# Attention in a fused kernel: normalising two steps later, the first round of products with values in two parts, weight conversions in other steps

## The chip, the cores and the metric

The kernel runs on one core of a Trainium2 chip. The metric is device time in microseconds (us) of one execution. Engines: TensorE (PE; PEld is its weight load), VectorE (DVE), ScalarE (ACT), GpSimd (POOL) and SyncE (SP), which issues DMA transfers. Each engine works through its own queue in order.

## What is computed

Threshold attention over 4 batches of 8 heads with 576 positions and a head width of 64, then two feed-forward layers over the 2304 tokens. Only the attention stands nearer here:

```python
scores = scale * np.matmul(q, k.transpose(0, 1, 3, 2))
thresh = np.max(scores, axis=-1, keepdims=True) - tau
scores = np.where(scores >= thresh, scores, -1000000000.0)
scores = scores - np.max(scores, axis=-1, keepdims=True)
attn = np.exp(scores)
attn = attn / (np.sum(attn, axis=-1, keepdims=True) + 1e-09)
return np.matmul(attn, v).astype(np.float32)
```

The feed-forward layers are `(1 / (1 + exp(-(x @ w_gate))) * (x @ w_val)) @ w_out` and a second one with a piecewise quadratic gate.

## The kernel before

Attention goes over 16 pairs of heads (`NP`). Each pair has five steps (`U` = 5): in steps 1 to 4 (`u` = 0 to 3) 128 queries of both heads, in step 5 (`u` = 4) the last 64 of both, through block-diagonal `corners`. The loop `for t in range(N + 9)` (L418) runs over all 80 steps and is a software pipeline: the code of one `t` issues parts of different steps.

- `scores(p, u)` (L243): TensorE writes the scores of step t into two PSUM tiles `wa` and `wb` (tile name w).
- `maxima` (L256): VectorE scales them into SBUF (tile s) and reduces them to the row maximum mx (L261); GpSimd adds tau to it (L264). The two PSUM tiles are free for the next scores once L261 has read them.
- `exponents` (L269): ScalarE, L273, tile ex.
- `masks` of step t - 1 (L276): VectorE compares, multiplies and sums (L281, tile p); GpSimd copies the last 64 columns into a tile lt (L288).
- `turns` of step t - 2 (L290): TensorE transposes p and lt (L298, L300, L317) into the PSUM tiles `wt` and `left`; `copies` (L322): ScalarE moves them into SBUF (tiles r and rl).
- `attend` (L343): the products with values, in two rounds. Round 0 takes the first 256 queries, round 1 the other 320; each is a sum over five chunks of 128 keys (the fifth is rl), in one PSUM tile `av`, which `drain` moves to `xall` on ScalarE (L359) after the last chunk. The table `rounds` (L412) says at which step after a pair's start which chunks of which round are issued; step 5 there is the first step of the next pair.
- The row sums are inverted (`denom`), transposed (L436), written to DRAM (`sum_rows`, L370) and read back on all partitions (`spread`, L376, tile rb) at the end of the tenth step after a pair's start. `normalise` (L378) multiplies `xall` by rb on GpSimd (L380), in two halves, in the twelfth and the thirteenth.

Beside that the loop converts the first feed-forward weights to single precision. `background` (L382) is a list of 43 pieces, one a call: an `extract` on ScalarE (L145) or one operation of VectorE on 128x512 elements (L155 to L169), and two loads ahead. L456 takes one piece in each of the second, third and fourth step of a pair up to step 62, and later yields a "gap" at the same places, in which the feed-forward part's first splits run on VectorE (L192, L506). L468 takes some extra ones.

No scheduler moves anything: each queue holds the work in the order in which the code issues it. At step 81 the loop yields to the feed-forward part, which issues its first weight loads (tile words, L129); TensorE's first products of that part follow (L514).

Of the kernel before, what the change touches and what calls it, by code (L numbers as in the profile page):

```python
# [29 lines left out]
def kernel(  # L30
# [21 lines left out]
    NP, _, S = q.shape  # L52
# [147 lines left out]
    def attention():  # L200
# [14 lines left out]
        U = nf + 1  # L215
# [27 lines left out]
        def scores(p, u):  # L243
            t = qk[p]
            for s in range(2):
                c = slice(s * HS, s * HS + HS)
                if u == nf:
                    nc.tensor.matmul(wa[:, s, :HS], corners[p % 2], t[:, 1, c], start=True, stop=True)
                    continue
                for e, w in enumerate((wa, wb)):  # L250
                    es = slice(e * D, e * D + D)
                    nc.tensor.matmul(  # L252
                        w[:, s, :HS], t[es, 0, u * P : u * P + P], t[es, 1, c], start=True, stop=True
                    )

        def maxima(p, u):  # L256

            t = sp.tile([P, 2, 2, HS], F32, tag="s", name="s")
            mx = mxs[(p * U + u) % 2]
            for e, w in enumerate((wa, wb)[: 1 if u == nf else 2]):  # L260
                nc.vector.tensor_scalar(  # L261
                    t[:, e], w[:, :, :HS], nscale, None, op0=ALU.mult, op1=ALU.min, accum_out=mx[:, 0, e : e + 1]
                )
                nc.gpsimd.tensor_scalar(  # L264
                    mx[:, 1, e : e + 1], mx[:, 0, e : e + 1], tau_b, None, op0=ALU.add
                )
            st[p, u] = t, mx

        def exponents(p, u):  # L269
            t, mx = st[p, u]  # L270
            ex = pe_.tile([P, 2, 2, HS], F32, tag="ex", name="ex")
            for e in range(1 if u == nf else 2):
                nc.scalar.activation(ex[:, e], t[:, e], AF.Exp, scale=-1.0, bias=mx[:, 0, e : e + 1])  # L273
            st[p, u] = t, mx, ex
# [15 lines left out]
        def turns(p, u):  # L290


            pr = pt.pop((p, u))
            if u == 2:
                for e in range(2):
                    for c in range(nf):
                        cs = slice(c * P, c * P + P)
                        nc.tensor.transpose(wt[:, e, cs], pr[:, e, cs], ident)  # L298
                for i in range(3):
                    nc.tensor.transpose(left[:, (i + 1) * P : (i + 2) * P], last(p, i), ident)  # L300
                return

            es = range(1 if u == nf else 2)
            todo = [(i * R, pr[:, e, c * P : c * P + P]) for i, (e, c) in enumerate(itertools.product(es, range(nf)))]
            if u == nf:
                todo.append((len(todo) * R, last(p, u)))
            for i, (o, x) in enumerate(todo):
                for h in range(2):
                    turn_half(wt[:, h, o : o + R], x, h)
                if u == 3 and i == 6:  # L310
                    turn_half(left[:, :R], last(p, 3, False), 0)
                if u == nf and i == 3:
                    turn_half(left[:, R:P], last(p, 3), 1)
# [8 lines left out]
        def copies(p, u):  # L322
            r, o = min(u // 2, 1), u % 2 * P if u < nf else 2 * P
            x = rt[r].rearrange("p e c n -> p (e c) n")
            if u == 2:
                nc.scalar.activation(x[:, :, o : o + P], wt.rearrange("p e (c n) -> p (e c) n", n=P), AF.Copy)
                nc.scalar.activation(rl[0], left[:, P : 3 * P], AF.Copy)
                nc.scalar.activation(rl[1][:, :P], left[:, 3 * P :], AF.Copy)
            elif u < nf:
                nc.scalar.activation(  # L330
                    x[:, :, o : o + P].rearrange("p m (h q) -> p h m q", h=2),
                    wt.rearrange("p h (m q) -> p h m q", q=R), AF.Copy,
                )
            else:
                nc.scalar.activation(
                    rt[r][:, :, :, o : o + R], wt[:, :, : nf * R].rearrange("p e (c q) -> p e c q", q=R), AF.Copy
                )
                nc.scalar.activation(rl[1][:, P : 2 * P], left[:, :P], AF.Copy)
                for e in range(2):
                    es = slice(e * R, e * R + R)  # L340
                    nc.scalar.activation(rl[1][es, o : o + R], wt[es, e, nf * R : (nf + 1) * R], AF.Copy)

        def attend(p, r, cs):  # L343


            n = NR[r]
            for c in cs:
                for e in range(2):
                    nc.tensor.matmul(  # L349
                        av[e * D : e * D + D, :n], vs[p % 3][:, e, c], rt[r][:, e, c] if c < nf else rl[r],  # L350
                        start=c == 0, stop=c == nf,
                    )

        def x_of(p):
            b, hp = divmod(p, NHP)
            return xall[:, hp, b * S : (b + 1) * S]
# [4 lines left out]
        def denom(p):  # L361
            rs = sums[p % 2]
            nc.vector.reciprocal(rs, rs)

        def sum_rows(p):

            n = 2 * nf + 1
            nc.scalar.activation(rows[p % 2][:n], left[:n, :P], AF.Copy)
            drs[p] = dram.tile([n, P], F32, tag="dr", name="dr")
            nc.sync.dma_start(out=drs[p], in_=rows[p % 2][:n])  # L370
# [7 lines left out]
        def normalise(p, s):  # L378
            x, c = x_of(p), slice(s * HS, s * HS + HS)
            nc.gpsimd.tensor_tensor(x[:, c], x[:, c], rbs[:, p % 2 * S :][:, c], op=ALU.mult)  # L380
# [28 lines left out]
        corner(0)  # L409
        bg = background()  # L410

        rounds = {6: (0, 0, 5), 7: (1, 0, 2), 8: (1, 2, 5)}  # L412
        final = {5: (0, 0, 5), 7: (1, 0, 5)}
        parts = {}
        for p in range(NP):
# [2 lines left out]
        for t in range(N + 9):  # L418
            p, u = divmod(t, U)
            on = t < N  # L420
            mk = divmod(t - 1, U) if 1 <= t <= N else None
            at = divmod(t - 2, U) if 2 <= t <= N + 1 else None

            pd, ud = divmod(t - U, U)
            pd2, ud2 = divmod(t - 2 * U, U)
            if ud2 in (2, 3) and 0 <= pd2 < NP:
                normalise(pd2, ud2 - 2)
            if on:
                scores(p, u)
            if t == N + 1:  # L430
                yield t - N, True
            if at:
                turns(*at)
            turned = 0 <= pd < NP and ud == (4 if pd + 1 < NP else 2)
            if turned:
                nc.tensor.transpose(left[: 2 * nf + 1, :P], sums[pd % 2], ident)  # L436
            for part in parts.get(t, ()):
                attend(*part)
            if on:
                maxima(p, u)  # L440
            if at:
                copies(*at)
            if on:
                exponents(p, u)
            if ud == 1 and 0 <= pd < NP:
                denom(pd)
            if turned:
                sum_rows(pd)
            for part in parts.get(t, ()):
                if part[2][-1] == nf:  # L450
                    drain(*part[:2])
            if mk:
                masks(*mk)
                if mk[1] == nf:
                    nc.gpsimd.tensor_scalar(sums[mk[0] % 2], sums[mk[0] % 2], 1e-9, None, op0=ALU.add)
            if on and u in (1, 2, 3) and t > 2:  # L456
                if t <= 12 * U + 2:
                    next(bg, None)
                else:
                    yield t - N, "gap"  # L460
            if on:
                if u == 1 and p + 1 < NP:
                    corner(p + 1)
                if u == 2 and p + 2 < NP:
                    load(p + 2)
                if u == 4 and p + 2 < NP:
                    load_v(p + 2)
                if t == 1 or u == 2 and p % 2 == 0 and p < 12:  # L468
                    next(bg, None)
            if ud2 == 0 and 0 <= pd2 < NP - 1:  # L470
                spread(pd2)
            if t == N + 3:
                spread(NP - 1)
            if t == N - 1:
                wides[:] = [wb, wa, wt]
            if t == N:
                run(bg)
                nc.scalar.activation(dummy, half, AF.Sigmoid)
                st1.close()
            if t == N + 2:  # L480
                st2.close()
                ps_o.close()
            yield t - N, False
# [497 lines left out]
```

## Time and profile before

| | us |
|---|---|
| median of 3 runs | 1131.78 |
| lowest and highest | 1131.24, 1133.29 |
| profiled execution | 1130.95 |
| its span | 1129.2 |

| engine | busy us | share of span |
|---|---|---|
| PE | 1098.9 | 97% |
| PEld | 943.8 | 84% |
| DVE | 851.0 | 75% |
| ACT | 617.9 | 55% |
| POOL | 144.9 | 13% |

Busy times are sums over the whole span, and attention is only its first quarter. The ends of matmuls are modelled, so a busy PE may be waiting inside a group. A wait is put down to whatever released it last.

### The profile page before, as it was taken

To read this page: it belongs to the slowest core of one execution; us is meant where nothing else is said; L and a number is where in the kernel's file an instruction comes from. 1 tells how busy PE (TensorE), PEld (TensorE's weight loads), DVE (VectorE), ACT (ScalarE), POOL (GpSimd) and SP (SyncE) were. 2 spreads that over 40 slices of the span, in tenths; PEclk is the share of its full clock that TensorE was granted. 3 is DMA by queue.
4 is the path that set the end of the run, shared out by engine and by line. 5 is a ranking of instruction groups with operands and counts; after the bars stand their busy time and mean duration, and the time that the engine had idled before them with its cause. 6 is when DMAs were issued, how large, how long until landed. Compare 5 with 4: busy or idle time off the path is not lost.

```text
span 1129.2 us, 18218 instructions
## 1 busy us (share of the span) xinstructions
PE 1098.9 (97%) x6852; PEld 943.8 (84%) x6852; DVE 851.0 (75%) x1484; ACT 617.9 (55%) x1016; POOL 144.9 (13%) x315
## 2 busy tenths in 40 slices
PE   8999999999899999999999999989999999999998
PEld 5666666566799999999999999979888888998887
DVE  6999999996799998776687653476767767776663
ACT  5777777777444335333344232365656665666553
POOL 3455554554100000000000000000000000000000
PEclk9999999999999999999999999999999999999999
DMA  4243442321756655544544533033321433143301
GB/s 153 62 89 84 84 99 62 74 58 24 254 187 199 208 197 214 187 152 172 189 163 157 176 137 117 9 112 112 112 99 70 168 112 113 70 153 114 112 19 57
DMA packets 65145, 139.16 MB, mean 123 GB/s; under 512 B 9616, under 2 KB 35872, under 8 KB 65056
## 3 DMA queue, kind: packets, MB, share of 16 engines
q1 hardware_dynamic: 64912, 137.98, 37.8%
q8 instruction: 54, 0.88, 0.3%
q14 instruction: 35, 0.29, 0.1%
q10 hardware_dynamic: 144, 0.00, 0.0%
HBM read 111.15 MB, written 26.81 MB: 122 GB/s over the span
## 4 chain that ended last, share of the span: by engine, by line
PE 75%; DVE 9%; DMA 7%; issue 4%; ACT 3%; POOL 2%; SPq 1%; DVEq 0%; POOLq 0%; ACTq 0%
PE y L772 15%; PE pu L639 14%; PE y L790 13%; PE pgv L515 8%; PE pgv L514 8%; PE pgv L516 8%; DMA rb<-dr 5%; PE w L252 5%; DVE p L281 3%; PE av L349 2%; DVE s L261 2%; DMA words<-in_moe_w_out_dram 2%; PE w L317 1%; SPq L129 1%; ACT sqs L648 1%
## 5 line engine op out<-in xcount | busy, mean ns | idle before, releaser
L514 PE MATMUL pgv<-xflat,win 128*128 128x384 f32 x560 | 188.0, 336 | 5.4 <-ACT act L570 4.7
L772 PE MATMUL y<-wout,hh 128*128 128x512 f32 x576 | 185.3, 397 | 3.0 <-ACT hh L657 3.0
L515 PE MATMUL pgv<-xflat,win 128*128 128x384 f32 x560 | 187.9, 335 | 0.1
L516 PE MATMUL pgv<-xflat,win 128*128 128x384 f32 x560 | 187.9, 336 | 0.0
L790 PE MATMUL y<-hh,wout 128*128 128x512 f32 (+1 forms) x576 | 146.5, 336 | 0.0
L772 PEld LDWEIGHTS y<-wout,hh 128*128 128x128 f32 x576 | 108.9, 189 | 28.0 <-ACT hh L657 3.3
L261 DVE TENSOR_SCALAR_CACHE_REDUCE s<-w,nscale 128x576 f32<-128x576 f32 x144 | 112.4, 813 | 19.4 <-PE w L252 15.0
L281 DVE SCALAR_TENSOR_TENSOR p<-s,mx,ex 128x576 f32<-128x576 f32 x144 | 115.3, 833 | 0.9 <-POOL mx L264 0.8
L772 PE MATMUL y<-wout,hl 128*128 128x512 f32 x288 | 114.4, 397 | 0.5 <-DVE hl L658 0.5
L574 DVE TENSOR_TENSOR act<-pgv,act 128x384 f32<-128x384 f32 x70 | 38.8, 554 | 98.5 <-PE pgv L516 98.2
L514 PEld LDWEIGHTS pgv<-xflat,win 128*128 128x128 f32 x560 | 105.5, 188 | 8.0 <-ACT act L570 5.4
L273 ACT ACTIVATE ex<-s,mx 128x576 f32<-128x576 f32 x144 | 104.5, 768 | 8.0 <-DVE s L261 7.4
L575 ACT ACTIVATE hh<-act 128x384 fp32r<-128x384 f32 x72 | 37.8, 525 | 128.8 <-DVE act L574 128.8
L790 PEld LDWEIGHTS y<-hh,wout 128*128 128x128 f32 x576 | 98.0, 188 | 11.3
L515 PEld LDWEIGHTS pgv<-xflat,win 128*128 128x128 f32 x560 | 105.5, 188 | 2.0 <-DVE xflat L506 0.4
L639 PE MATMUL pu<-xflat,win 128*128 128x384 f32 x576 | 105.3, 337 | 1.0 <-DVE sqs L718 0.7
L516 PEld LDWEIGHTS pgv<-xflat,win 128*128 128x128 f32 x560 | 105.5, 188 | 0.0
L639 PEld LDWEIGHTS pu<-xflat,win 128*128 128x128 f32 x576 | 100.9, 188 | 2.4 <-DVE sqs L718 1.4
L570 ACT ACTIVATE act<-pgv 128x384 f32<-128x384 f32 x70 | 34.0, 486 | 118.9 <-PE pgv L516 118.6
L252 PE MATMUL w<-qk 64*128 64x288 f32 x512 | 93.2, 435 | 4.1 <-DVE s L261 3.5
L790 PE MATMUL y<-hl,wout 128*128 128x512 f32 (+1 forms) x288 | 97.1, 337 | 0.0
L252 PEld LDWEIGHTS w<-qk 64*128 64x128 f32 x512 | 49.6, 187 | 38.5 <-DVE s L261 24.2
(149 smaller groups left out, 1925.6 us busy)
## 6 DMA issues: line engine op xcount, KB each, us to landing
wmore<-saved SPq DMA_DIRECT2D x32, 512.0 KB
words<-in_moe_w_out_dram SPq DMA_DIRECT2D x26, 512.0 KB
tsum<-tsaved SPq DMA_DIRECT2D x24, 512.0 KB
wmore<-saved SPq DMA_DIRECT2D x15, 768.0 KB
words<-in_moe_w_in_dram SPq DMA_DIRECT2D x16, 512.0 KB
saved<-w SPq DMA_DIRECT2D x16, 512.0 KB
w<-saved SPq DMA_DIRECT2D x16, 512.0 KB
w<-saved SPq DMA_DIRECT2D x9, 768.0 KB
```

The source lines that it names most:

```text
L252: nc.tensor.matmul(w[:, s, :HS], t[es, 0, u * P : u * P + P], t[es, 1, c], start=True, stop=True)
L261: nc.vector.tensor_scalar(t[:, e], w[:, :, :HS], nscale, None, op0=ALU.mult, op1=ALU.min, accum_out=mx[:, 0, e : e + 1])
L273: nc.scalar.activation(ex[:, e], t[:, e], AF.Exp, scale=-1.0, bias=mx[:, 0, e : e + 1])
L281: nc.vector.scalar_tensor_tensor(pr[:, e], t[:, e].rearrange("p a b -> p (a b)"), mx[:, 1, e : e + 1], ex[:, e].rearrange("p a b -> p (a b ...
L514: nc.tensor.matmul(ps, ih[:, i, kk], xh[:, kk, c], start=(kk == 0), stop=False)
L515: nc.tensor.matmul(ps, ih[:, i, kk], xl[:, kk, c], start=False, stop=False)
L516: nc.tensor.matmul(ps, il[:, i, kk], xh[:, kk, c], start=False, stop=(kk == KD - 1))
L574: nc.vector.tensor_tensor(act, pv, act, op=ALU.mult)
L575: nc.scalar.activation(hh[:, c], act, AF.Copy)
L639: nc.tensor.matmul(ps[bank], l[:, k], r[:, k], start=bool(new) and k == m == 0, stop=k == HK - 1 and m == 2, skip_group_check=True,)
L772: nc.tensor.matmul(y[b], l[:, ts_], r, start=first and m == 0, stop=last and m == 2)
L790: nc.tensor.matmul(at(y, a, b), l[:, ds_], r[:, c], start=new and m == 0, stop=last and m == 2, skip_group_check=True,)
```

## The change

The first round of products with values is issued in two parts: chunks 1 and 2 in the first step of the next pair (5), chunks 3 to 5 in the second (6). `normalise` is issued 14 and 15 steps after a pair's start in place of 12 and 13, but for the last two pairs, which keep 12 and 13. The pieces of `background` and the gaps are taken in the first, fourth and fifth step of a pair, up to step 60.

```diff
--- before.py
+++ after.py
@@ -409,7 +409,7 @@
         corner(0)
         bg = background()
 
-        rounds = {6: (0, 0, 5), 7: (1, 0, 2), 8: (1, 2, 5)}
+        rounds = {5: (0, 0, 2), 6: (0, 2, 5), 7: (1, 0, 2), 8: (1, 2, 5)}
         final = {5: (0, 0, 5), 7: (1, 0, 5)}
         parts = {}
         for p in range(NP):
@@ -423,8 +423,11 @@
 
             pd, ud = divmod(t - U, U)
             pd2, ud2 = divmod(t - 2 * U, U)
-            if ud2 in (2, 3) and 0 <= pd2 < NP:
-                normalise(pd2, ud2 - 2)
+            for i in range(2):
+                for j in (12, 14):
+                    pn, un = divmod(t - j - i, U)
+                    if un == 0 and 0 <= pn < NP and (pn < NP - 2) == (j == 14):
+                        normalise(pn, i)
             if on:
                 scores(p, u)
             if t == N + 1:
@@ -453,8 +456,8 @@
                 masks(*mk)
                 if mk[1] == nf:
                     nc.gpsimd.tensor_scalar(sums[mk[0] % 2], sums[mk[0] % 2], 1e-9, None, op0=ALU.add)
-            if on and u in (1, 2, 3) and t > 2:
-                if t <= 12 * U + 2:
+            if on and u in (0, 3, 4) and t > 2:
+                if t <= 12 * U:
                     next(bg, None)
                 else:
                     yield t - N, "gap"
```

TensorE, first pair: from the end of the first step's transposes to the second step's products (r_163 is the transposed p of round 0, rl_165 its fifth chunk, v_167 the values, w_126 and w_127 the score tiles).

```order
@@ -29,4 +29,5 @@
 L317 MATMUL left<-ident,lt 128x64
 L317 MATMUL w_128<-ident,p 128x64 x2
+L349 MATMUL av<-r_163,v_167 64x256 x4
 L252 MATMUL w_126<-qk 128x288
 L252 MATMUL w_127<-qk 128x288
@@ -36,5 +37,5 @@
 L317 MATMUL left<-ident,lt 128x64
 L317 MATMUL w_128<-ident,lt 128x64 x2
-L349 MATMUL av<-r_163,v_167 64x256 x8
+L349 MATMUL av<-r_163,v_167 64x256 x4
 L349 MATMUL av<-rl_165,v_167 64x256 x2
```

Two of the five chunks (four matmuls, for two heads) now stand ahead of the second step's scores.

GpSimd, from the second step of the third pair: before,

```order
L241 COPY corner_0_74<-qk_661 64x64 x2
L380 TENSOR_TENSOR xall_72<-xall_72,rb_73 128x288
L264 TENSOR_SCALAR mx_1_77<-mx_1_77,tau_b_68 128x1 x2
L288 COPY lt_864<-p_861 128x128
L380 TENSOR_TENSOR xall_72<-xall_72,rb_73 128x288
L264 TENSOR_SCALAR mx_0_76<-mx_0_76,tau_b_68 128x1 x2
L288 COPY lt_910<-p_907 128x128
```

and now:

```order
L241 COPY corner_0_74<-qk_660 64x64 x2
L264 TENSOR_SCALAR mx_1_77<-mx_1_77,tau_b_68 128x1 x2
L288 COPY lt_864<-p_861 128x128
L264 TENSOR_SCALAR mx_0_76<-mx_0_76,tau_b_68 128x1 x2
L288 COPY lt_908<-p_905 128x128
L380 TENSOR_TENSOR xall_72<-xall_72,rb_73 128x288
L264 TENSOR_SCALAR mx_1_77<-mx_1_77,tau_b_68 128x1
L288 COPY lt_940<-p_937 128x128
L380 TENSOR_TENSOR xall_72<-xall_72,rb_73 128x288
L264 TENSOR_SCALAR mx_0_76<-mx_0_76,tau_b_68 128x1 x2
```

The two multiplications (L380) stood ahead of the thresholds (L264) of the third and fourth step; now they stand ahead of those of the fifth step (the row with a single mx) and of the next first step.

VectorE, from the mask of a fifth step through the second step behind it: before,

```order
L281 SCALAR_TENSOR_TENSOR p_773,sum_0_80<-s_723,mx_0_76,ex_729 128x576
L261 TENSOR_SCALAR s_805,mx_0_76<-w0_126,nscale_69 128x576
L261 TENSOR_SCALAR s_805,mx_0_76<-w1_127,nscale_69 128x576
L363 RECIPROCAL sum_0_80<-sum_0_80 128x9
L281 SCALAR_TENSOR_TENSOR p_819,sum_1_81<-s_764,mx_1_77,ex_770 128x576 x2
L157 TENSOR_SCALAR w32_0_82<-high0_84 128x512
L261 TENSOR_SCALAR s_852,mx_1_77<-w0_126,nscale_69 128x576
L261 TENSOR_SCALAR s_852,mx_1_77<-w1_127,nscale_69 128x576
L281 SCALAR_TENSOR_TENSOR p_861,sum_1_81<-s_805,mx_0_76,ex_814 128x576 x2
L159 SCALAR_TENSOR_TENSOR w32_0_82<-high0_84,w32_0_82 128x512
```

and now, from the masks of a fourth step on:

```order
L281 SCALAR_TENSOR_TENSOR p_733,sum_0_80<-s_691,mx_1_77,ex_697 128x576 x2
L157 TENSOR_SCALAR w32_0_82<-high0_84 128x512
L261 TENSOR_SCALAR s_769,mx_1_77<-w0_126,nscale_69 128x576
L261 TENSOR_SCALAR s_769,mx_1_77<-w1_127,nscale_69 128x576
L281 SCALAR_TENSOR_TENSOR p_778,sum_0_80<-s_722,mx_0_76,ex_728 128x576
L159 SCALAR_TENSOR_TENSOR w32_0_82<-high0_84,w32_0_82 128x512
L261 TENSOR_SCALAR s_807,mx_0_76<-w0_126,nscale_69 128x576
L261 TENSOR_SCALAR s_807,mx_0_76<-w1_127,nscale_69 128x576
L363 RECIPROCAL sum_0_80<-sum_0_80 128x9
L281 SCALAR_TENSOR_TENSOR p_821,sum_1_81<-s_769,mx_1_77,ex_775 128x576 x2
```

The conversions L157 and L159 stood behind the masks of the second and third step; now they stand behind the masks issued in the fifth and the first.

## Rows read from the trace of the kernel before

**Rows 1.** The page's chain that ended last: shares of the span by engine, by line.

```profile
PE 75%; DVE 9%; DMA 7%; issue 4%; ACT 3%; POOL 2%; SPq 1%; DVEq 0%; POOLq 0%; ACTq 0%
PE y L772 15%; PE pu L639 14%; PE y L790 13%; PE pgv L515 8%; PE pgv L514 8%; PE pgv L516 8%; DMA rb<-dr 5%; PE w L252 5%; DVE p L281 3%; PE av L349 2%; DVE s L261 2%; DMA words<-in_moe_w_out_dram 2%; PE w L317 1%; SPq L129 1%; ACT sqs L648 1%
```

**Rows 2.** Busy times by pair from each second step on; the first line names the columns.

```profile
core 0: us, PE busy (x) PEld busy (x) DVE busy (x) ACT busy (x) POOL busy (x), PEclk, DMA share, GB/s
...
156.21:172.80 16.59, 16.23 (x149) 10.49 (x149) 15.48 (x41) 12.44 (x23) 8.79 (x19) 1.00 0.39 72
...
sum 250.82, PE 239.49 PEld 155.76 DVE 234.42 ACT 195.75 POOL 132.24; mean PE 15.97 PEld 10.38 DVE 15.63 ACT 13.05 POOL 8.82
```

**Rows 3.** Waits of VectorE, 23.18 to 274.0: waiter, releaser, total us, times, longest.

```profile
DVE s L261 <- PE w L252: 11.5, 16, 1.1
DVE p L281 <- POOL mx L264: 0.8, 2, 0.4
```

**Rows 4.** Waits of TensorE in the same stretch.

```profile
PE left L300 <- POOL lt L288: 5.1, 7, 1.0
PE w L252 <- DVE s L261: 1.7, 8, 0.3
```

**Rows 5.** Waits of GpSimd in the same stretch.

```profile
POOL xall L380 <- DMA rb<-dr: 52.3, 17, 4.7
```

**Rows 6.** Groups of instructions, VectorE, same stretch: count, busy us, mean ns, idle before.

```profile
L281 DVE SCALAR_TENSOR_TENSOR p<-s,mx,ex 128x576 f32<-128x576 f32 x136 | 109.1, 834 | 0.9 <-POOL mx L264 0.8
L155 DVE TENSOR_SCALAR high<-high 128x512 f32<-128x512 f32 x5 | 4.5, 891 | 0.0
L161 DVE TENSOR_SCALAR high<-w 128x512 uint32<-128x512 uint32 x6 | 3.7, 614 | 0.0
L157 DVE TENSOR_SCALAR w<-high 128x512 uint32<-128x512 uint32 x6 | 2.5, 418 | 0.0
```

**Rows 7.** Timeline of one pair: start us, us, engine, line, what, idle before.

```profile
155.68 0.33 PE L317 MATMUL w<-ident,p 64*128 64x64 f32 x2
...
156.81 0.81 DVE L281 SCALAR_TENSOR_TENSOR p<-s,mx,ex 128x576 f32<-128x576 f32 x1
...
158.47 1.95 PE L349 MATMUL av<-r,v 128*64 128x256 f32 x16
...
160.78 1.24 PE L252 MATMUL w<-qk 64*128 64x288 f32 x8
...
162.05 0.82 DVE L261 TENSOR_SCALAR_CACHE_REDUCE s<-w,nscale 128x576 f32<-128x576 f32 x1 [0.85 <-PE w L252]
...
165.01 0.68 DVE L159 SCALAR_TENSOR_TENSOR w<-high,w 128x512 uint32<-128x512 uint32 x1
...
165.62 0.81 DVE L261 TENSOR_SCALAR_CACHE_REDUCE s<-w,nscale 128x576 f32<-128x576 f32 x1
```

**Rows 8.** Timeline: GpSimd, and what runs or waits beside it.

```profile
157.76 0.29 POOL L288 COPY lt<-p 128x128 f32<-128x128 f32 x1
...
165.51 0.84 POOL L380 TENSOR_TENSOR xall<-xall,rb 128x288 f32<-128x288 f32 x1 [3.70 <-DMA rb<-dr]
...
167.07 0.81 POOL L380 TENSOR_TENSOR xall<-xall,rb 128x288 f32<-128x288 f32 x1
...
167.09 1.40 DVE L281 SCALAR_TENSOR_TENSOR p<-s,mx,ex 128x576 f32<-128x576 f32 x1
...
172.36 0.14 PEld L317 LDWEIGHTS left<-ident,lt 64*128 64x128 f32 x1 [0.25 <-POOL lt L288]
...
228.10 0.95 DVE L506 TENSOR_TENSOR xflat<-xall,xflat 128x768 fp32r<-128x768 f32 x1
...
228.31 0.89 POOL L288 COPY lt<-p 128x128 f32<-128x128 f32 x1 [0.73 <-PE av L349]
```

**Rows 9.** Timeline: the end of attention, the feed-forward part's first load and first product.

```profile
275.98 2.98 SPq L129 DMA_DIRECT2D words<-in_moe_w_gate_dram  x1
...
276.43 0.44 PE L514 MATMUL w<-xflat,win 128*128 128x384 f32 x1
```

## The prediction

> **What bounds the kernel now.** The change touches only the attention loop, so the first question is which part of the span is attention. It runs from the start to 276 us: there SyncE issues the first weight loads of the feed-forward part and TensorE its first product of that part [rows 9]. Both are released by the end of attention, and what follows hangs on these loads and products. I therefore take it that a microsecond won before 276 us is a microsecond at the end. The chain of waits agrees that attention has something to give: 5% of the span is the load of the broadcast reciprocals (rb) and another 5% or so VectorE's masks and maxima [rows 1].
>
> Inside attention I read the busy times by pair of heads. From the second step of the second pair to the same place behind the sixteenth there are 15 pairs in 250.82 us, 16.72 us each. TensorE shows 239.49 us busy, VectorE 234.42, ScalarE 195.75, GpSimd 132.24 [rows 2]. So two engines are nearly full and pass work to each other: scores to maxima, masks to transposes. VectorE's account is the easier one to keep, since its busy time is not modelled: 250.82 - 234.42 = 16.4 us idle. Next, what ends that idle time. VectorE waited 11.5 us, 16 times, for scores, and 0.8 us for GpSimd's threshold (mx) [rows 3]; the other 4 us are short gaps of 0.2 us between a mask and a maximum. TensorE waited 5.1 us for GpSimd's copies (lt) and 1.7 us for VectorE to free the score banks [rows 4]. GpSimd stood 52.3 us behind rb [rows 5], and its mx and lt stand behind that in the same queue.
>
> The place of the 11.5 us is seen in one pair. In the second step 20 records of the products with values begin at 158.47 and the next scores only at 160.78; VectorE takes these up at 162.05 after a wait of 0.85 us, 1.27 us after they began [rows 7]. Nearly every pair has such a wait: 16 of them, 0.7 us on average, the longest 1.1 [rows 3].
>
> **Part 1: products with values in two parts.** Eight of the 20 records go from the second step to the first. The 20 take 160.78 - 158.47 = 2.31 us, so eight take 0.92. The third step's scores can start 0.92 us sooner behind the second step's, which is more than the 0.85 that VectorE waited: the 11.5 us go. **-11.5 us.**
>
> The eight records now stand ahead of the second step's scores. Is VectorE there first? In the pair shown the first step's transposes end at 155.68 + 0.33 = 156.01 [rows 7]. Scores behind 0.92 of products start at 156.93 and reach VectorE 1.27 later, at 158.20. VectorE ends its mask (0.81 from 156.81) at 157.6 and then has, new there, a conversion: 165.62 - 165.01 = 0.61 us. It comes at 158.2. That is level, with no reserve. One thing pushes TensorE later: GpSimd's lt copy of the step before now has a conversion beside it. Alone the copy took 0.29 us; beside an operation of VectorE with two inputs, 0.89 [rows 8]. TensorE already waited 0.25 us for such a copy in the first step [rows 8], so up to 0.6 us more falls on it, while VectorE is itself later by the same conversion, of 0.34 to 0.61 us. I take 0.3 us of new wait per pair, the middle of 0 (VectorE as late as TensorE) and 0.6: 15 x 0.3. **+4.5 us**, ends 0 and 9.
>
> **Part 2: conversions in steps one, four and five.** Their number does not change; the loop condition ends two steps sooner and the same list of operations is spread over it. VectorE's work stays. In the second and third step it has less to do, in the first and fifth more, and that cost is the cover counted above. Of the feed-forward splits that take the same places once the conversions are done, the same holds; there are seven, and one of the longer took 0.95 us [rows 8]. The loads of the weights that go with a conversion are issued behind the query and key loads as before; SyncE's queue is the same row for row. Cost of its own: nothing, if the short gaps between mask and maximum only change places (0.2 us at the ends of two steps either way); 0.2 x 15 = 3 us either way if they do not.
>
> **Part 3: normalising two steps later.** The two multiplications of a pair move from the third and fourth step of the pair after next to its fifth and the one behind it. On GpSimd's queue the first is moved past four mx and two lt, the second past three mx and two lt. GpSimd's 52.3 us of waiting [rows 5] was seldom on the path, but where it was it made VectorE wait 0.8 us [rows 3] and TensorE 5.1 [rows 4]. Two steps are two fifths of a pair, 6.7 us, longer than the longest of those waits, 4.7 [rows 5], so I count rb as always landed. **-0.8 us** on VectorE's account; TensorE's 5.1 lies beside VectorE's work and is not counted twice.
>
> The multiplications do not vanish, and beside them VectorE is slower: a mask took 1.40 us where a normalise ran, against 0.81 [rows 8, 7]; a maximum that began while another ran, at 165.62, kept 0.81 [rows 7, 8]. How much that was in all: masks 136 x (0.834 - 0.81) = 3.3 us, L155 5 x (0.891 - 0.418) = 2.4, L161 6 x (0.614 - 0.418) = 1.2, taking L157's mean for an undisturbed one [rows 6]; 6.9 us together. After the change each multiplication follows an lt copy, and VectorE's next operations are a short conversion and then maxima, which do not suffer. No row shows this order. Ends: 0, and every one of the 28 stretching an operation by 1.40 - 0.81 = 0.59, 16.5 us. I take half of the present sum, 3.5, since what runs beside it is nearest to the undisturbed maximum at 165.62. **-3.4 us.**
>
> The Trainium skill has a rule against this part and part 2 (page "SBUF — State Buffer", section "SBUF: two separate sides"): VectorE and GpSimd share a pair of ports under an exclusive lock, and an operation of VectorE with two SBUF inputs blocks one of GpSimd that reads SBUF for its whole length, and the reverse. The 1.40 us mask and the 0.89 us copy agree with it; that a maximum, which reads PSUM, kept 0.81 does too. By it alone every copy placed beside a conversion is late by the whole conversion, which is the second rival.
>
> **Sum.** -11.5 + 4.5 - 0.8 - 3.4 = -11.2 us, 0.75 us per pair. The profiled execution took 1130.95 us (span 1129.2); less 11.2 that is 1119.75. The median of the runs shown is 0.83 above it, so 1120.6.
>
> **Rivals.**
> 1. TensorE is the bound. If its 239.49 us are a floor, only 11.3 us are there for it, and what the change clearly frees is its waits for lt and for the score banks, 5.1 + 1.7 = 6.8 us [rows 4]: 1125.0. For it: TensorE is busier than VectorE in the sum. Against: those busy times are stretched by waits inside a group, as the scores that reach VectorE 1.27 us after their start everywhere. The Trainium skill ("Perfetto Trace Analysis", section "Identifying the Most-Contended Engine") says that matmul busy time is no good measure, and weight-load busy time is; here that is 155.76 of 250.82 us [rows 2], which speaks against this rival as well. Chance 0.17.
> 2. Slower: the lt copies become the path. Conversions now stand in the steps after which TensorE at once transposes the copy, in the first step and the second. If each copy is late by the whole 0.61 us conversion and TensorE, and behind it VectorE, waits for it, the price is 2 x 0.61 x 15 = 18.3 us in place of 4.5: -11.5 - 0.8 - 3.4 + 18.3 = +2.6, 1134.4. It decides from the point where TensorE reaches the copy's transpose before the copy is there, and VectorE has no mask left to do meanwhile. The 0.25 us wait [rows 8] says that the first half holds; the mask and conversion of the first step speak against the second. Chance 0.09.
> 3. The normalise collides with masks and conversions in its new place 28 times: -11.5 + 4.5 - 0.8 + (16.5 - 6.9) = +1.8, 1133.6, hardly a difference. Chance 0.10.
> 4. No new wait in the second step: -11.5 - 0.8 - 3.4 = -15.7, 1116.1; without any stretching 1112.6. VectorE would be full. Chance 0.14.
>
> **How the numbers follow.** My forecast, 1120.6, has 0.50 and by the ends of the new wait (0 to 9) and the gaps a range of its own of 1116.5 to 1125.5. To hold 8 in 10 I add rival 1 and most of rival 4: 1113.5 to 1129.0; outside lie rivals 2 and 3, 0.19. A difference of 0.2% (2.3 us) is about what a measurement of this kernel can tell from none. Faster: 0.50 + 0.17 + 0.14 = 0.81; the same: rival 3, 0.10; slower: rival 2, 0.09.
>
> **What would show it.** In the trace after: 15 pairs in some 239.6 us instead of 250.8. VectorE's waits for scores (rows 3) fall from 11.5 to about 4.5 us and lie in the second step rather than the third. GpSimd's wait for rb is gone but for the last two pairs, whose multiplications stay where they are, and TensorE's wait for lt before L300 with it. Mean mask duration falls towards 0.82. The prediction is wrong in part 1 if waits for scores stay near 11 us, in part 3 if masks or conversions get longer on average, and in its first step if attention ends sooner but the feed-forward part takes longer.

## The result

The changed kernel takes 1113.68 us (median of 4 runs, 1113.31 to 1113.98), beside 1131.94 before: the ratio of the runs is 0.9837 with a 95% interval of 0.9820 to 0.9854, that is 16.5 to 20.4 us less. The forecast was 11.2 us less, 1120.6, with a range that began at 1113.5. Against the 1131.78 that the forecast started from, the ratio gives 1113.3, just under that range. The sign and the engine to watch were right. The size was not, and the part that was given most of the gain gives little by itself.

The page of the changed kernel (its span is 1112.0 us): the busy times, and the chain that ended last, by engine.

```profile
PE 1086.4 (98%) x6852; PEld 939.8 (85%) x6852; DVE 844.0 (76%) x1484; ACT 616.5 (55%) x1016; POOL 152.7 (14%) x315
...
PE 67%; DVE 4%; ACT 2%; DMA 1%; issue 1%; SPq 1%; POOL 0%; DVEq 0%; ACTq 0%; POOLq 0%
```

In [rows 1] the load of rb had 5% of the span on that chain. This chain cannot be set beside it: its shares add up to 76%, since, followed back, it breaks off at 255 us, near the end of attention. Whether rb is still on the path is read from the waits below and from the runs.

Where the time went is read from the account of VectorE over the attention part, from the first scores to the feed-forward part's first weight load. The columns are those of [rows 2], the core's five engines each with its busy us and its number of instructions. The first fence is the kernel before, the second the kernel after.

```profile
5.90:275.98 270.08, 255.66 (x2335) 166.28 (x2336) 249.19 (x635) 207.41 (x358) 138.98 (x298) 1.00 0.34 78
```

```profile
5.90:259.21 253.31, 243.08 (x2335) 162.43 (x2336) 241.78 (x635) 205.93 (x358) 146.72 (x298) 1.00 0.36 83
```

The stretch is 270.08 - 253.31 = 16.8 us shorter. VectorE's busy time fell by 249.19 - 241.78 = 7.4 us for the same 635 instructions, and its idle time from 20.9 to 11.5 us, by 9.4. What follows attention starts that much sooner; the counterparts of [rows 9] in the timeline after:

```profile
259.21 3.19 SPq L129 DMA_DIRECT2D words<-in_moe_w_gate_dram  x1
...
259.53 0.44 PE L517 MATMUL w<-xflat,win 128*128 128x384 f32 x1
```

Next VectorE's waits in the pairs (waiter, releaser, total us, times, longest), which answer to [rows 3]:

```profile
DVE s L261 <- PE w L252: 2.6, 10, 0.3
DVE s L261 <- PE w L248: 0.3, 1, 0.3
```

11.5 us of waits for scores have become 2.6, and the 0.8 for mx are gone. The groups of VectorE's instructions in the same stretch (busy us, mean ns, idle before), which answer to [rows 6]:

```profile
L281 DVE SCALAR_TENSOR_TENSOR p<-s,mx,ex 128x576 f32<-128x576 f32 x136 | 105.7, 811 | 0.0
...
L161 DVE TENSOR_SCALAR high<-w 128x512 uint32<-128x512 uint32 x6 | 2.5, 421 | 0.0
L155 DVE TENSOR_SCALAR high<-high 128x512 f32<-128x512 f32 x5 | 2.1, 419 | 0.0
```

Masks fell from 834 to 811 ns on average, L161 from 614 to 421, L155 from 891 to 419. So of the stretching beside the multiplications nothing is left that these means show. GpSimd's waits, in place of [rows 5]:

```profile
POOL mx L264 <- DVE s L261: 48.4, 107, 0.8
POOL lt L288 <- DVE p L281: 27.8, 38, 0.7
POOL lt L288 <- PE w L252: 16.4, 22, 1.0
```

rb is no longer among them. And TensorE's, in place of [rows 4]: the wait for lt before L300 is gone, and there is one for ScalarE's copy of the row sums.

```profile
PE left L317 <- ACT row L368: 4.8, 12, 0.4
```

One pair of the changed kernel shows all three parts at work (start us, us, engine, line, what, idle before).

```profile
144.12 0.82 DVE L261 TENSOR_SCALAR_CACHE_REDUCE s<-w,nscale 128x576 f32<-128x576 f32 x1
144.25 0.79 POOL L380 TENSOR_TENSOR xall<-xall,rb 128x288 f32<-128x288 f32 x1
...
144.86 0.81 DVE L281 SCALAR_TENSOR_TENSOR p<-s,mx,ex 128x576 f32<-128x576 f32 x1
...
146.68 0.81 DVE L261 TENSOR_SCALAR_CACHE_REDUCE s<-w,nscale 128x576 f32<-128x576 f32 x1
146.88 0.79 POOL L380 TENSOR_TENSOR xall<-xall,rb 128x288 f32<-128x288 f32 x1
...
147.62 1.08 PE L349 MATMUL av<-r,v 128*64 128x256 f32 x8
...
148.64 1.24 PE L252 MATMUL w<-qk 64*128 64x288 f32 x8
...
148.89 0.69 DVE L159 SCALAR_TENSOR_TENSOR w<-high,w 128x512 uint32<-128x512 uint32 x1
...
149.91 0.82 DVE L261 TENSOR_SCALAR_CACHE_REDUCE s<-w,nscale 128x576 f32<-128x576 f32 x1 [0.33 <-PE w L252]
...
150.18 1.08 PE L349 MATMUL av<-r,v 128*64 128x256 f32 x8
...
151.62 1.24 PE L252 MATMUL w<-qk 64*128 64x288 f32 x8
...
152.20 0.82 DVE L281 SCALAR_TENSOR_TENSOR p<-s,mx,ex 128x576 f32<-128x576 f32 x1
...
153.15 0.82 DVE L261 TENSOR_SCALAR_CACHE_REDUCE s<-w,nscale 128x576 f32<-128x576 f32 x1
```

Both multiplications (L380 at 144.25 and 146.88) run beside a maximum (L261 at 144.12 and 146.68) and take 0.79 us; the maxima keep 0.82 and 0.81. The first products (147.62) stand ahead of the second step's scores (148.64), for which VectorE, its conversion L159 done, waits 0.33 us at 149.91. The second part (150.18) lets the third step's scores begin at 151.62; VectorE takes them up at 153.15, straight behind its mask (152.20), where before it waited 0.85 us [rows 7].

### The profile page after: what moved, and what is told of

Read it like the earlier page. It is cut to its first block, busy times and chain, and to the rows that moved or that the text cites. A ratio compares the mean times of both kernels' runs of the same rounds, so it can differ in the third digit from the quotient of the medians.

```text
span 1112.0 us, 18232 instructions
## 1 busy us (share of the span) xinstructions
PE 1086.4 (98%) x6852; PEld 939.8 (85%) x6852; DVE 844.0 (76%) x1484; ACT 616.5 (55%) x1016; POOL 152.7 (14%) x315
## 4 chain that ended last, share of the span: by engine, by line
PE 67%; DVE 4%; ACT 2%; DMA 1%; issue 1%; SPq 1%; POOL 0%; DVEq 0%; ACTq 0%; POOLq 0%
PE y L775 15%; PE pu L642 15%; PE y L793 13%; PE pgv L517 8%; PE pgv L518 8%; PE pgv L519 8%; DMA words<-in_moe_w_out_dram 1%; SPq L129 1%; DMA dr<-row 1%; ACT sqs L651 1%; ACT sqs L652 1%; ACT hh L660 1%; DVE vals L658 0%; DVE ssum L610 0%; DVE high L165 0%
## 5 line engine op out<-in xcount | busy, mean ns | idle before, releaser
L261 DVE TENSOR_SCALAR_CACHE_REDUCE s<-w,nscale 128x576 f32<-128x576 f32 x144 | 112.6, 816 | 10.9 <-PE w L252 6.2
L281 DVE SCALAR_TENSOR_TENSOR p<-s,mx,ex 128x576 f32<-128x576 f32 x144 | 111.9, 811 | 0.0
L264 POOL TENSOR_SCALAR mx<-mx,tau_b 128x1 f32<-128x1 f32 x144 | 87.4, 607 | 57.7 <-DVE s L261 56.8
L252 PE MATMUL w<-qk 64*128 64x288 f32 x512 | 82.6, 432 | 2.0 <-DVE s L261 1.9
```

The source lines that it names most:

```text
L252: nc.tensor.matmul(w[:, s, :HS], t[es, 0, u * P : u * P + P], t[es, 1, c], start=True, stop=True)
L261: nc.vector.tensor_scalar(t[:, e], w[:, :, :HS], nscale, None, op0=ALU.mult, op1=ALU.min, accum_out=mx[:, 0, e : e + 1])
L264: nc.gpsimd.tensor_scalar(mx[:, 1, e : e + 1], mx[:, 0, e : e + 1], tau_b, None, op0=ALU.add)
L281: nc.vector.scalar_tensor_tensor(pr[:, e], t[:, e].rearrange("p a b -> p (a b)"), mx[:, 1, e : e + 1], ex[:, e].rearrange("p a b -> p (a b ...
```

## The experiments

The theory held at the start was the forecast's: VectorE's account, in which the products in two parts carry most. Its main rival came from the chain: the wait for rb, which stands ahead of the thresholds and the copies in GpSimd's queue, carries most. Each part can be undone alone, so all combinations were run. "Less" is against the kernel before, run beside them.

| products in two parts | conversions moved | normalising later | us | less | ratio (95%) |
|---|---|---|---|---|---|
| x | | | 1129.63 | 2.8 | 0.9971 to 0.9990 |
| | x | | 1133.94 | -1.6 | 1.0009 to 1.0028 |
| | | x | 1121.44 | 11.0 | 0.9895 to 0.9925 |
| x | x | | 1131.37 | 0.6 | 0.9980 to 1.0000 |
| x | | x | 1118.09 | 14.3 | 0.9865 to 0.9895 |
| | x | x | 1124.93 | 7.1 | 0.9919 to 0.9949 |
| x | x | x | 1113.68 | 18.3 | 0.9820 to 0.9854 |

**Products alone.**

```diff
-        rounds = {6: (0, 0, 5), 7: (1, 0, 2), 8: (1, 2, 5)}
+        rounds = {5: (0, 0, 2), 6: (0, 2, 5), 7: (1, 0, 2), 8: (1, 2, 5)}
```

> Of the three parts only the first: the first round's products with values in two parts of 2 and 3 chunks; conversions and normalising as before. Theory A (VectorE is the bound, and its account is waits for scores plus operations stretched beside the normalise): the waits for scores in the third step (11.5 us) go, but the second step's scores now stand behind 0.92 us of products with no conversion in the first step as cover, so some 0.6 us per pair comes back there: 2 to 5 us faster, 1127 to 1130, masks still 0.83 us on average. Rival B (the parts are independent, and this one carries the gain): 9 us or more faster, below 1123.

1129.63 us, as theory A had it; rival B falls. VectorE's waits:

```profile
DVE s L261 <- PE w L252: 9.8, 15, 0.8
DVE p L281 <- POOL mx L264: 3.4, 3, 1.7
```

Waits for scores are still 9.8 us, all of them now in the second step, and those for mx have risen from 0.8 to 3.4.

**Conversions alone.**

```diff
-            if on and u in (1, 2, 3) and t > 2:
-                if t <= 12 * U + 2:
+            if on and u in (0, 3, 4) and t > 2:
+                if t <= 12 * U:
```

> Only the second part: conversions in the first, fourth and fifth step. Theory A: in the second step they lay ahead of VectorE's wait for the third step's scores and cost nothing; taken away there, that wait grows by as much, and in the first and fifth step they add to VectorE's work: 3 to 8 us slower, 1135 to 1140, waits for scores 15 us or more. Rival B (where the conversions stand does not matter): within 2 us of 1131.8.

1133.94 us, 1.6 us slower, and the interval leaves out no change; the sign is that of theory A, the size under its 3 to 8 and about at rival B's 2. The conversions had filled time ahead of the late scores, and without them VectorE waits longer there:

```profile
DVE s L261 <- PE w L252: 16.7, 15, 1.1
DVE p L281 <- POOL mx L264: 2.2, 3, 1.2
```

**Normalising alone.**

```diff
-            if ud2 in (2, 3) and 0 <= pd2 < NP:
-                normalise(pd2, ud2 - 2)
+            for i in range(2):
+                for j in (12, 14):
+                    pn, un = divmod(t - j - i, U)
+                    if un == 0 and 0 <= pn < NP and (pn < NP - 2) == (j == 14):
+                        normalise(pn, i)
```

> Only the third part: normalising two steps later. Theory A: GpSimd no longer waits for rb, masks fall from 0.834 to about 0.81 us on average and the slow conversions to 0.42, some 7 us of VectorE's time, but part of it turns into waits for scores in the third step, which stay: 3 to 7 us faster, 1125 to 1129. Rival B (TensorE's waits for lt behind rb are what the part frees): about 5 us faster with masks still at 0.83. Rival C (the whole gain is in this part): below 1117.

1121.44 us: 11.0 us, more than any theory allowed but rival C, which wanted still more. The account and the waits:

```profile
5.90:266.35 260.45, 252.09 (x2331) 167.41 (x2332) 241.94 (x635) 206.57 (x358) 144.50 (x298) 1.00 0.35 81
```

```profile
DVE s L261 <- PE w L252: 10.4, 15, 0.9
```

The account says where, for 9.6 of the 11.0 us: 7.25 us less busy (249.19 to 241.94), 2.4 us less idle (20.9 to 18.5). Waits for scores stay at 10.4 us, as theory A said; that some of the freed time would turn into more of them did not happen. The chain of this kernel does reach back to the start, and the load of rb, 5% in [rows 1], is not among its lines:

```profile
PE y L775 15%; PE pu L642 15%; PE y L793 13%; PE pgv L518 8%; PE pgv L517 8%; PE pgv L519 8%; PE w L252 6%; PE av L349 5%; DVE p L281 4%; DVE s L261 3%; PE w L317 2%; DMA words<-in_moe_w_gate_dram 1%; ACT sqs L651 1%; ACT sqs L652 1%; SPq L129 1%
```

**Two parts of three.** Normalising where it was:

> First and second part, normalising where it was. Theory A: what the third part is worth with the others in place is missing, the stretched operations and the waits behind rb: 6 to 9 us slower than the changed kernel, 1120 to 1123, with masks at 0.83 us and GpSimd's wait for rb at some 50 us. Rival B (the place of normalising only moves work that is hidden): within 2 us of 1113.7.

1131.37 us. This was the surprise: the two parts to which the forecast gave 11.5 - 4.5 = 7.0 us give 0.6 without the third. Theory A's 1120 to 1123 falls, and rival B, that the place of normalising is hidden, is 17.7 us off. VectorE's waits tell why, and below them its account:

```profile
DVE p L281 <- POOL mx L264: 11.4, 13, 1.6
DVE s L261 <- PE w L252: 4.4, 16, 1.1
```

```profile
5.90:277.26 271.36, 249.20 (x2333) 161.68 (x2334) 249.03 (x635) 207.76 (x358) 146.67 (x298) 1.00 0.34 77
```

The waits for scores are down to 4.4 us. That this is so near the forecast's 4.5 is chance: the forecast had put them in the second step, and here 13 of the 16 are waits of 0.23 to 0.26 us in the third, hardly more than the gap of 0.2 us that stands between a mask and a maximum anyway. But the waits for mx rose from 0.8 to 11.4. And VectorE's busy time did not fall. The masks took 0.81 us, not theory A's 0.83; more of the stretching now fell on two of the conversions (L161 took 0.61 and L155 0.89 us before [rows 6], and 0.42 undisturbed):

```profile
L281 DVE SCALAR_TENSOR_TENSOR p<-s,mx,ex 128x576 f32<-128x576 f32 x124 | 96.2, 808 | 11.4 <-POOL mx L264 11.4
...
L161 DVE TENSOR_SCALAR high<-w 128x512 uint32<-128x512 uint32 x6 | 5.5, 910 | 0.0
L155 DVE TENSOR_SCALAR high<-high 128x512 f32<-128x512 f32 x5 | 5.0, 1009 | 0.0
```

In one pair of that kernel:

```profile
142.72 1.11 SPq L376 DMA_DIRECT2D rb<-dr  x2
...
150.34 0.81 DVE L261 TENSOR_SCALAR_CACHE_REDUCE s<-w,nscale 128x576 f32<-128x576 f32 x1
150.37 0.80 POOL L380 TENSOR_TENSOR xall<-xall,rb 128x288 f32<-128x288 f32 x1 [3.28 <-DMA rb<-dr]
...
151.15 0.55 POOL L264 TENSOR_SCALAR mx<-mx,tau_b 128x1 f32<-128x1 f32 x2
151.48 0.82 DVE L281 SCALAR_TENSOR_TENSOR p<-s,mx,ex 128x576 f32<-128x576 f32 x1 [0.32 <-POOL mx L264]
...
152.22 0.83 DVE L281 SCALAR_TENSOR_TENSOR p<-s,mx,ex 128x576 f32<-128x576 f32 x1
...
152.41 1.30 POOL L380 TENSOR_TENSOR xall<-xall,rb 128x288 f32<-128x288 f32 x1
...
152.99 1.01 DVE L155 TENSOR_SCALAR high<-high 128x512 f32<-128x512 f32 x1
...
154.36 0.28 POOL L288 COPY lt<-p 128x128 f32<-128x128 f32 x1
...
154.69 0.33 PE L300 MATMUL left<-ident,lt 128*128 128x128 f32 x1 [0.69 <-POOL lt L288]
```

The load of rb is issued at 142.72. The first multiplication starts when it has landed, 7.65 us later, after 3.28 us in which GpSimd stood still. Behind it come the thresholds (151.15), for which VectorE's mask waits until 151.48. The second multiplication begins beside the next mask (152.22) and takes 1.30 us; the conversion behind that mask, L155, takes 1.01. The next lt copy, which stands behind the multiplication in GpSimd's queue, runs only at 154.36, and TensorE waits 0.69 us for it. From the issue of the load to the first multiplication it was 7.4 to 8.2 us in the first 13 pairs of this kernel, and 7.3 to 7.7 in the kernel before: this flight does not get shorter when the steps beside it do. VectorE had lost that time waiting for scores; take that wait away and it waits for mx.

The other two combinations:

> First and third part, conversions as before. Theory A: all of the gain but for the cover that the conversions give in the first step: 10 to 14 us faster than before, 1118 to 1122, with waits for scores of some 6 to 9 us in the second step. Rival B (the conversions' place is worth nothing): as the changed kernel, 1113.7.

1118.09 us, as theory A had it. The waits for scores are 10.3 us, above its 6 to 9, and all in the second step. The second fence shows one of them: scores behind the first products, with no conversion as cover, cost 0.68 us.

```profile
DVE s L261 <- PE w L252: 10.3, 15, 0.8
```

```profile
150.63 0.82 DVE L261 TENSOR_SCALAR_CACHE_REDUCE s<-w,nscale 128x576 f32<-128x576 f32 x1 [0.68 <-PE w L252]
```

> Second and third part, the products in one part. Theory A: the third step's scores stay late and the conversion that filled the time ahead of them is gone: 1127 to 1134, with waits for scores of 13 us or more in the third step. Rival B (the products' split is a small part): below 1120.

1124.93 us, between the two expectations, 2.1 us under theory A's; the waits are those of theory A:

```profile
DVE s L261 <- PE w L252: 16.9, 16, 1.1
```

So conversions and products belong together: with normalising later, products alone add 3.4 us (1121.44 to 1118.09), conversions alone take 3.5 (1124.93), both add 7.8 (1113.68).

**Wait or work?** These leave the multiplications out:

```diff
         def normalise(p, s):
             x, c = x_of(p), slice(s * HS, s * HS + HS)
-            nc.gpsimd.tensor_tensor(x[:, c], x[:, c], rbs[:, p % 2 * S :][:, c], op=ALU.mult)
+            return
```

> The kernel before without the multiplications of normalise (the attention's division is left out; rb is still loaded). Theory A: the stretched operations and the queue behind rb are gone at their source, so it is as fast as the third part alone, within 1.5 us. Rival B (the third part only moves part of the cost to another place): 3 us or more faster than the third part alone.

1120.76 us, ratio 0.9896 (0.9881 to 0.9911), beside 1121.44 and 0.9910 for normalising later alone; the intervals overlap, as theory A had it.

> The changed kernel without the multiplications of normalise (the attention's division is left out; rb is still loaded). Theory A: in their new place they lie beside maxima and cost next to nothing: within 1 us of 1113.7. Rival B (half of the stretching is still there, as forecast): 3 us or more faster than the changed kernel.

1112.65 us (0.9812 to 0.9841), 1.0 us under the changed kernel, with overlapping intervals: in the new place the multiplications cost about that or nothing. Rival B, which was the forecast's own half of the stretching, falls. The next pair keeps the multiplications and their places, and takes away what they wait for:

```diff
+    ones = const.tile([P, HS], F32, name="ones")
...
+        nc.gpsimd.memset(ones, 1.0)
...
-            nc.gpsimd.tensor_tensor(x[:, c], x[:, c], rbs[:, p % 2 * S :][:, c], op=ALU.mult)
+            nc.gpsimd.tensor_tensor(x[:, c], x[:, c], ones, op=ALU.mult)
```

> The kernel before with normalise multiplying by a constant tile of ones in place of rb (the division is left out; rb is still loaded): the same GpSimd instructions at the same places in its queue, with nothing to wait for. It tells waiting for rb from colliding. Theory A1 (the wait for rb is what costs, and moves the multiplications beside masks): as fast as without the multiplications. Theory A2 (colliding costs at any place beside masks): no faster than 2 us below the kernel before, masks at 0.83 us.

1121.15 us, ratio 0.9909 (0.9892 to 0.9925), beside 0.9896 for leaving them out: theory A1. The waits for mx are gone, and the masks take 0.81 us, not theory A2's 0.83 (the lines are numbered one higher here):

```profile
L282 DVE SCALAR_TENSOR_TENSOR p<-s,mx,ex 128x576 f32<-128x576 f32 x131 | 101.5, 808 | 0.0
```

At the old place, without the wait, the multiplications cost nothing that these runs can tell. So the collisions too came from the wait: it made the multiplications start at a time set by the load, wherever VectorE then was.

> First and second part, normalise at its old place but multiplying by a constant tile of ones in place of rb (the division is left out; rb is still loaded). If it is the wait for rb that ate the gain of the first two parts (VectorE's waits for mx, 11.4 us there), this is as fast as the changed kernel: 1112.5 to 1115, waits for mx gone. If it is the place in GpSimd's queue: 1120 or more.

1114.15 us (0.9827 to 0.9853), beside 1112.62 for the changed kernel in the same company. The waits for mx are gone and those for scores are 3.3 us (again one line higher):

```profile
DVE s L262 <- PE w L253: 3.0, 12, 0.3
DVE s L262 <- PE w L249: 0.3, 1, 0.3
```

With the wait for rb away, products and conversions give nearly all of their worth at the old place of normalising: attention takes 253.5 us there and 253.3 in the changed kernel. So it was the wait, and not the place in the queue, that had eaten their gain. The 1.5 us that this kernel is slower as a whole stay unexplained.

**One step later.**

```diff
-                for j in (12, 14):
+                for j in (12, 13):
...
-                    if un == 0 and 0 <= pn < NP and (pn < NP - 2) == (j == 14):
+                    if un == 0 and 0 <= pn < NP and (pn < NP - 2) == (j == 13):
```

> The changed kernel with normalising one step later than before rather than two (thirteenth and fourteenth step after a pair's start). rb has 3.3 us more than before. Theory A: rb lands before or little after, and the multiplications stand ahead of the fourth and fifth step's thresholds, each again behind an lt copy and beside maxima: 1113.5 to 1116. Rival B (only the second later step frees the queue): 1118 or more.

1117.72 us (0.9866 to 0.9895), 4 us slower than two steps: a little under rival B's 1118, and outside theory A. GpSimd's wait for rb is 9.1 us, and the masks take 854 ns, more than in the kernel before:

```profile
POOL xall L380 <- DMA rb<-dr: 9.1, 10, 1.5
```

```profile
L281 DVE SCALAR_TENSOR_TENSOR p<-s,mx,ex 128x576 f32<-128x576 f32 x133 | 109.2, 854 | 0.0
```

> Normalising one step later than before, products and conversions as in the changed kernel, multiplying by a constant in place of rb (the division is left out; rb is still loaded). If the 4 us that one step later lacks against two steps come from the last wait for rb (9.1 us, 10 times), which starts the multiplications beside masks: 1113 to 1114.5, masks back from 0.854 to 0.81 us. If they come from the place in the queue itself: 1117 to 1118, masks at 0.85.

1114.64 us (0.9831 to 0.9858), with the masks at 0.809 us. This is 0.1 over the expected range; of the 4 us some 3 go with the wait, and whether the rest (2.0 us to the changed kernel beside it) is the place is open.

**What bounds it now.** ScalarE's copy of the row sums ahead of the exponents:

```diff
+            if turned:
+                sum_rows(pd)
             if on:
                 exponents(p, u)
             if ud == 1 and 0 <= pd < NP:
                 denom(pd)
-            if turned:
-                sum_rows(pd)
```

> The changed kernel with ScalarE's copy of the transposed row sums issued ahead of the exponents of the same step instead of behind them. TensorE's waits for that copy (4.8 us, 12 times 0.4) should go. If they are on the path through the second step's scores, VectorE's waits for scores (2.6 us) go with them: 1111 to 1113. If VectorE is full anyway: within 0.5 us of 1113.7.

1111.10 us (0.9807 to 0.9836). TensorE's 4.8 us of waits for the copy are gone; what is left at that place is 1.8 us, in 7 waits, for lt. VectorE's waits for scores did not go with them: they are 3.9 us, in 17 waits, where the changed kernel has 2.6 in 10.

Since the intervals of this and the changed kernel overlap, both were run side by side.

> The changed kernel once more, as the neighbour of the next run: 1113.7.

> ScalarE's copy of the row sums ahead of the exponents, on the same chip as the changed kernel: 2 to 3 us faster than it if the copy is on the path, within 1 us if not.

1112.62 us (1112.43 to 1113.41; 0.9815 to 0.9842) for the changed kernel, 1112.11 (1110.64 to 1112.43; 0.9807 to 0.9833) with the copy first. It is the faster of the two in both comparisons, and in both traces attention ends sooner with it (at 256.0 and 255.9 us, in place of 259.2 and 258.5). But the 0.5 us here are within the 1 us that was to mean that the copy is not on the path, and less than can be told apart: whether it beats the changed kernel stays open.

## Why the prediction was off

**Attention's gain passes through: right.** The first weight load came 16.8 us sooner, the whole profiled execution 17.2 (1130.95 to 1113.74).

**Products, -11.5 and +4.5: right in the changed kernel, but only there.** The wait in the third step went. The new one in the second came in 5 of the 15 pairs, 0.33 us each and 1.7 in all, of 2.9 us that are left of waits for scores. That lies inside the ends of 0 and 9; the 4.5 was the middle between them and no reading. On its own the edit gave 2.8 us: without the conversions as cover 9.8 us of waits came back in the second step, and the waits for mx rose to 3.4.

**Conversions, nothing of their own (3 us either way): right in no combination.** Alone they cost 1.6 us, with normalising later 3.5; beside the products and normalising later they gain 4.4 (1118.09 to 1113.68). The forecast said that they are the cover for the products, which is this gain, but gave no price without it.

**Normalising, -0.8 and -3.4: here the forecast failed**, in two ways. The term of the stretching was mis-sized: half of 6.9 us was taken, all 7.4 went. The text had the reason, that maxima do not suffer, and did not follow it: behind an lt copy the next operations of VectorE are mostly maxima, and both multiplications of the pair shown ran beside one. That is 4.0 of the missing 5.6 us; the other 1.6 are waits for scores, 2.6 and 0.3 in place of 4.5. And the step "seldom on the path" was wrong in kind. The 0.8 us of VectorE's wait for mx was the price of the wait for rb only as long as another wait ended later; with that one gone it was 11.4. The chain of [rows 1] had given the load of rb 5% of the span; the forecast went by the list of waits. Normalising later is worth 11.0 us by itself, where 4.2 were forecast, and 17.7 with the other two parts in place (1131.37 to 1113.68). In the sum for all three parts this step did little harm, since each of VectorE's waits stood in it once and all of them went. The share of each part was far off: 7.0 forecast for products and conversions without it, 0.6 measured.

**Rivals.** TensorE as the bound (1125.0) falls: its busy time in attention fell from 255.66 to 243.08 us, so it was no floor. The lt copies as the path fall too: TensorE's waits for lt came to 0.7 us. They are late where the order puts them beside a conversion with two inputs: in the changed kernel a copy that began at 162.12 beside L165 (0.69 us from 161.91) took 0.62 us, and TensorE was then still held by the row copy. This agrees with the rule in the Trainium skill's "SBUF — State Buffer" ("SBUF: two separate sides"), that an operation of VectorE with two SBUF inputs blocks one of GpSimd that reads SBUF. Collisions in the new place fall with the 1.0 us of the run without the multiplications. The fourth rival, no new wait and up to no stretching (1116.1 to 1112.6), came nearest; its second half, no stretching, is what the runs show, while a smaller new wait is there.

## What to carry to other kernels

A wait on an in-order queue ahead of something that others need has a price that the list of waits shows only in part: as long as a second wait ends later, the first seems free, and removing the second alone gave next to nothing here (0.6 us of 18.3). So when two engines are nearly full, ask of each wait that is removed which one ends next in the same step, and run the edits in combination before one is called useless. Where a multiplication on GpSimd disturbs VectorE, look first at what sets its start: here a load did, and once the operand was there in time the queue itself placed it beside work that does not mind.

## What the runs showed that was not expected

The flight of rb, from issue to the first multiplication that waits for it, was 7.3 to 7.7 us in the kernel before and 7.4 to 8.2 with products and conversions changed. A multiplication beside a maximum (PSUM to SBUF) ran its 0.79 us and left the maximum at 0.82. One that began beside a mask (two inputs in SBUF), with a conversion of one input behind that mask (L155), took 1.30 us; the mask kept 0.83 us, and the conversion took 1.01 in place of 0.42. So the same multiplications cost VectorE stretched masks and conversions in the kernel before, stretched conversions with products and conversions changed, and nothing that can be told in the changed kernel, by what runs when they start.
